# Three side steps per 18 gated products, a longer estimate for one load, and a weight set split in other places

## The chip, the core and the metric

The kernel runs on one core of one Trainium2 chip. The core has five engines that work side by side, each from its own queue, in order: TensorE (PE, matrix products; PEld is its weight load), VectorE (DVE), ScalarE (ACT), GpSimd (POOL) and SyncE (SP, which here issues transfers only). The metric is the device time of one execution in microseconds, the median of several runs; lower is better.

## The reference, cut

```python
# q, k, v: (4, 12, 448, 64)
scores = cap * np.tanh(q @ k.T / np.sqrt(64) / cap)
attn = np.exp(scores - scores.max(-1)); attn /= attn.sum(-1) + 1e-9
x = (attn @ v)                 # as (1792, 768)
x = ((x @ w1) * (x @ w2)) @ w3 @ w_out        # gated: w1, w2 768x1024, w3 1024x1024
h = x @ w_in                   # 768x1024
sm = softmax(h); solu = h * sm
ln = (solu - mean) / np.sqrt(var + 1e-6) * g_ln
out = ln @ w_out2              # 1024x768
```

All is float32. A product of two float32 numbers is made of three products of a high and a low half ("h", "l" in names): a cast makes the high half, a subtraction the low one. So every operand and weight tile has to be split before TensorE may use it.

## The kernel before

**Stages.** The attention runs over 24 pairs of heads (names sc, p, o, n). Beside it TensorE multiplies weights with weights: w3, w_out and w_in become one matrix, stored as w_dr (names f). Then come the gated products (names ab, wt, xs): for each of eight blocks f of the inner width, weights w_f come in three pieces (landing in ld, converted on VectorE by L328, L331, L334 into cv, cast by L340, the low half by L349), and tokens of four batches b are multiplied with them. The gated products begin beside the attention and go on after it. Six blocks of the gated products for the last two batches are made by a scheme of seven products for eight (L1332, names us, ys, vs; block n, product j; weights q). The last two stages use the same scheme for the folded matrix (L1432, weights ws, one tile for each of the seven sets; operands a) and for the output (weights wg).

**What sets the order.** In the attention a planner (class Order) writes the order of all engines: every step has an engine, a rank, a time on that engine and a time until its result is there, and is put in the queue when the planner's clock says so. Side work waits in two lists: `ahead` (weights) and `xq` (tokens). For the tokens, `plan_x` loads the row sums' inverses rb from DRAM by GpSimd (L830), VectorE scales by them (L843), the results are cast and split. The numbers behind `("pool", ...)` on the line that ends `plan_x` are the planner's time for the issue and until the load has landed, in ns.

After the attention the planner stops. The rest of the gated products runs in a plain loop: `fill(18 * 201)` gives TensorE 18 products, then `ahead.step(n)` takes n steps of the side list, `xq.step(1)` one of the tokens. This part alone is left to a scheduler, which orders what is recorded there by its own model. The blocks behind it are in a fixed order again: `plan(n, j, ...)` puts side work behind product j of block n. `finish` copies us to p1s, u2s, p7s on ScalarE (L1336) and adds on VectorE (L1339).

**Names of the change.** `EARLY` is the order (1, 2, 6, 7, 5) of the weight sets; `EARLY[1]` is set 2, tile ws2, loaded by `block_load` and split into high and low halves by `plan_block` (L340, L349) or by `high_w` and `low_w` (L1372, L1376). `high(r, m)` takes a buffer for operand m of row block r and makes the high half; for m of 3, 4 and 5 the buffers are three of one tag, dealt in the order in which they are asked for. They lie where tiles of the stage before lay, so the first use of each waits until its former tile is read.

Of the kernel before, what the change touches and what calls it, by code (L numbers as in the profile page):

```python
# [10 lines left out]
F32R = mybir.dt.float32r  # L11
# [7 lines left out]
P = 128  # L19
# [6 lines left out]
HALF = 512  # L26
# [17 lines left out]
EARLY, LATE = (1, 2, 6, 7, 5), (4, 3)  # L44
# [197 lines left out]
def attention_moe_solu(ctx: ExitStack, tc: tile.TileContext, q, k, v, cap, w12, w3t, wo, win, wout2, g_ln, out):  # L242
# [9 lines left out]
    pe, act, dve, pool, sync = nc.tensor, nc.scalar, nc.vector, nc.gpsimd, nc.sync  # L252
# [567 lines left out]
    def plan_x(b, parts=range(NPAIR // 2)):  # L820
        for part in parts:
            i = len(xq.items)
            pairs = slice(2 * part, 2 * part + 2)
            one, open_ = [], since(lambda b=b, part=part: free_x(b, part))

            def load(i=i, pairs=pairs):
                rb[i] = early.tile([P, 2, S], F32, tag="rb", name=f"rb{i}")
                for j in range(2):
                    row = r_dr[b].rearrange("(n j) s -> j n s", j=2)[j:j + 1, pairs]
                    pool.dma_start(out=rb[i][j * D:(j + 1) * D], in_=row.to_broadcast([D, 2, S]))  # L830

            def begin(part=part, one=one):

                for c in (2 * part, 2 * part + 1):
                    xs[b, c] = place_x(b, c)
                one.append(raw(xs[b, 2 * part + 1][:, 0, :1]))
                pool.memset(one[0], 1.0)

            def scale(i=i, part=part, one=one):
                two, *each = xr[b, part]  # L840
                by = rb.pop(i)
                for x, y in ([(two, by)] if two is not None else [(x, by[:, k]) for k, x in enumerate(each)]):
                    dve.scalar_tensor_tensor(x, x, one[0], y, ALU.mult, ALU.mult)  # L843

            def first(begin=begin, scale=scale):
                return [("pool", 0, 120, 300, begin), ("dve", 2, 1090, 1230, scale)]

            def rest(part=part):
                (_, *x), steps = xr.pop((b, part)), []
                if b == 3:  # L850
                    whole[part] = x
                for i in range(2):
                    to = xs[b, 2 * part + i]
                    steps.append(("any", 1, copying(S), None, lambda e, to=to, i=i: cast(to[:, 0], x[i], e)))
                for i in range(2):
                    to = xs[b, 2 * part + i]
                    steps.append(("dve", 2, 560, 680, lambda to=to, i=i: low(to[:, 0], to[:, 1], x[i])))
                slot = held_at.pop(("xr", b, part))
                return steps + [("none", 0, 0, 0, lambda: ring["xr"].give(slot, order.time))]

            def there(b=b, part=part, open_=open_):
                times = stored.get((b, part)), open_()
                return None if None in times else max(times)
            xq.add(("x", b, part), load, first, rest, None, there, ("pool", 1300, 5200))

# [45 lines left out]
    def block_load(m, part, dr, t_dr, dst):  # L913
        sync.dma_start(out=raw(dst[:, 1, rows(part), :]), in_=block_src(m, part, dr, t_dr))
# [5 lines left out]
    def second(m):  # L920
        if m not in ws:
            ws[m] = both_.tile([P, 2, NF // 2, HALF], F32R, tag="many", name=f"ws{m}")
        return ws[m]

    def plan_block(m, part):
        there = since(lambda: "ws" in place)
        ahead.add(("f", m, part), lambda: block_load(m, part, W4, tw_dr, second(m)), list,
                  lambda: [("none", 0, 0, 0, lambda: block_split(ws[m], part))], None, there)
# [79 lines left out]
    def plan_plain(key, do, test, load=lambda: None):  # L1008
        ahead.add(key, load, list, lambda: [("none", 0, 0, 0, do)], None, since(test))
# [64 lines left out]
    plan_tg(4, 5, 6, 7)  # L1074
    for c in range(NC // 2):
        plan_plain(("U", c), lambda c=c: one_four(c), lambda: (NF - 1, 1) in fin)
    for part in range(2):
        plan_block(EARLY[1], part)
    plan_plain("set1", lambda: None, lambda: (NF, PASSES[1][1]) in fin, lambda: load_set(1))

    def gated_tile(t):
# [221 lines left out]
    opened(right, "below", "right").tile([P, 16], F32, name="below")  # L1303
    place["set"], place["ts"] = opened(right, "set", "right"), opened(right, "ts", "right")
    while fill(18 * 201):
        ahead.step(2)
        xq.step(1)
    while xq.step(1):
        pass
# [7 lines left out]
    def plan(n, j, *entries):  # L1317
        for f, *args in entries:
            side.setdefault((n, j), []).append(lambda f=f, args=args: f(*args))
# [58 lines left out]
    for n in range(AGAIN):  # L1378
        follows = n + 1 < AGAIN
        if n:  # L1380
            plan(n, 0, (combine_low, n, 3))
        plan(n, 0, (low12, n, 6), (high12, n, 3))
        plan(n, 1, (low12, n, 7), (low12, n, 5), (low12, n, 3))
        if follows:
            plan(n, 2, (combine, n + 1, 7))
            plan(n, 3, (combine_low, n + 1, 7), (combine, n + 1, 5))
            plan(n, 4, (combine_low, n + 1, 5), (combine, n + 1, 6), (high12, n + 1, 7))
            plan(n, 5, (combine_low, n + 1, 6), (high12, n + 1, 5))
            plan(n, 6, (combine, n + 1, 3), (high12, n + 1, 6))
        if n + 2 < AGAIN:  # L1390
            for j, q in ((1, 0), (2, 1), (4, 2), (6, 3)):
                plan(n, j, (load_quarter, n + 2, q))
        plan(n, 6, (given, n, PASSES[1][0], "u2"))
    plan(LATER - 1, 0, (load_first,))
    plan(LATER, 0, (last_sets,), (load_ws, EARLY[2]), (load_ws, EARLY[3]))
    plan(LATER, 3, (first_operands,))
# [25 lines left out]
    side, both, taken = {}, {}, [2]  # L1422
# [119 lines left out]
    def source(r, m):  # L1542
        if m in (1, 6):
            return (x[r][0] if m == 1 else sums[r][2]).rearrange("p (a b) -> p a b", a=2)
        return {7: lambda: sums[0][3][:, HALF:], 5: lambda: sums[r][1], 4: lambda: quarter(r, 1, 1), 3: lambda: sums[r][4]}[m]()

    def high(r, m):
        if m in (1, 6, 7):
            t = op.tile([P, 2, 2, HALF], F32R, tag="two", bufs=3, name=f"a{r}_{m}")
            if m != 7:  # L1550
                a.setdefault(r, {}).update({m: t[:, 0], m + 1: t[:, 1]})
                both[r, m] = t[:, :, 0], t[:, :, 1]
            else:
                a[r][m] = t[:, 1]
                both[r, m] = t[:, 1, 0], t[:, 1, 1]
        else:
            a[r][m] = t = op.tile([P, 2, HALF], F32R, tag="one", bufs=3, name=f"a{r}_{m}")
            both[r, m] = t[:, 0], t[:, 1]
        act.copy(both[r, m][0], source(r, m))  # L1559

    def low(r, m):
# [51 lines left out]
        ws[EARLY[4]] = place["w567"].tile([P, 2, NF // 2, HALF], F32R, tag=f"w{EARLY[4]}", name=f"ws{EARLY[4]}")  # L1613

    plan(0, 0, (fifth,), (load_late, 5), (load_late, 4), (load_late, 3), (load, 1, 0), (load, 1, 1), (low_w, ws, 7, 0), (high_w, ws, 7, 1), (low_w, ws, 7, 1), (begun_sums,))
    plan(0, 1, (high, 0, 7), (low, 0, 7), (high, 0, 5), (low, 0, 5))
    plan(0, 3, (high_w, ws, 5, 0), (low_w, ws, 5, 0), (high_w, ws, 5, 1), (low_w, ws, 5, 1), (high, 0, 4), (high_w, ws, 4, 0), (sum4, 0))
    plan(0, 4, (low, 0, 4), (low_w, ws, 4, 0), (high_w, ws, 4, 1), (low_w, ws, 4, 1), (high, 0, 3), (high_w, ws, 3, 0))
    plan(0, 5, (low, 0, 3), (low_w, ws, 3, 0), (high_w, ws, 3, 1), (low_w, ws, 3, 1))
# [123 lines left out]
```

## Time and profile before

| | us |
|---|---|
| median of 3 runs (800.0 to 800.51) | 800.07 |
| the profiled execution, its own time | 805.94 |
| its span, first to last instruction | 804.2 |
| mean granted clock of TensorE, share of full speed | 0.985 |
| TensorE busy | 778.8 |
| VectorE busy | 617.6 |
| ScalarE busy | 440.8 |

The busy times come from one execution. TensorE's is close to the span, so a reader looks for the places where it stands still, and at the granted clock around them: after a pause TensorE may run at 1.2 instead of 2.4 GHz. Times in the rows below count from the span's start.

### The profile page before, as it was taken

Reading aid. Unit: us, or ns where it says so; the run is one execution under the profiler, and the core shown is the slowest. Engines: PE = TensorE matmul, PEld = TensorE weight load, DVE = VectorE, ACT = ScalarE, POOL = GpSimd, SP = SyncE. Lnnn points to the kernel's source line nnn. Section 1 sums busy time; section 2 is a strip of 40 time slices with the busy share of each in tenths; the row PEclk is TensorE's granted clock in tenths of the full one; section 3 lists DMA queues with packets and bytes.
Section 4 is the critical chain, followed back from the end, with each engine's and each line's share of the span. In section 5 each row is a group of like instructions: output and inputs, shape, how many; then the busy total and the mean of one; then the engine's idle time right before and its main releaser. Section 6 shows DMA issues by size and latency. Waiting matters only on the chain.

```text
span 804.2 us, 11305 instructions
## 1 busy us (share of the span) xinstructions
PE 778.8 (97%) x3956; PEld 617.6 (77%) x3956; DVE 617.6 (77%) x1134; ACT 440.8 (55%) x654; POOL 54.4 (7%) x106
## 2 busy tenths in 40 slices
PE   9999999999999998999986998999999999999998
PEld 6556666867766765777975997998688888899998
DVE  6995795799898668765776977787886668878973
ACT  6877766357487685672321312224576667755642
POOL 0110000001100111000100000000011111100000
PEclk9999999999999999999997998999999999999999
DMA  8776456677977765627968797463833335996532
GB/s 285 246 233 209 145 193 193 180 256 256 308 259 241 239 181 174 216 105 290 326 223 302 251 292 235 143 192 140 273 110 124 113 100 119 269 214 132 144 92 79
DMA packets 150936, 162.46 MB, mean 202 GB/s; under 512 B 66340, under 2 KB 122848, under 8 KB 149856
## 3 DMA queue, kind: packets, MB, share of 16 engines
q1 hardware_dynamic: 148144, 155.91, 61.2%
q0 software_dynamic: 2592, 5.73, 3.1%
q8 instruction: 31, 0.51, 0.3%
q14 instruction: 25, 0.20, 0.1%
q10 hardware_dynamic: 144, 0.10, 0.0%
HBM read 114.04 MB, written 47.53 MB: 201 GB/s over the span
## 4 chain that ended last, share of the span: by engine, by line
PE 74%; DMA 10%; DVE 8%; ACT 4%; issue 3%; SPq 0%; POOL 0%; DVEq 0%; ACTq 0%; POOLq 0%
PE u L1432 14%; PE ab L1120 8%; PE f L755 8%; PE o L523 7%; PE f L771 7%; PE v L1432 7%; PE sc L442 5%; PE us L1332 5%; PE y L1432 4%; DMA ld<-in_w 3%; PE vs L1332 2%; PE n L523 2%; PE sc L438 2%; DMA rb<-r_dr 2%; DMA tg_dr<-t 1%
## 5 line engine op out<-in xcount | busy, mean ns | idle before, releaser
L1120 PE MATMUL ab<-xs,wt 128*128 128x448 f32 x720 | 154.8, 374 | 10.1 <-ACT wt L340 9.8
L1120 PEld LDWEIGHTS ab<-xs,wt 128*128 128x128 f32 x720 | 138.7, 194 | 26.6 <-ACT wt L340 10.5
L455 ACT ACTIVATE sc<-sc,small 128x896 f32<-128x896 f32 (+1 forms) x96 | 82.8, 888 | 47.3 <-PE sc L442 40.6
L460 ACT ACTIVATE p<-sc,small 128x896 f32<-128x896 f32 (+1 forms) x96 | 84.3, 919 | 0.6
L1432 PE MATMUL u<-ws,a 128*128 128x512 f32 x336 | 80.8, 391 | 1.2 <-DVE ws L1376 0.9
L523 PE MATMUL o<-p,vd 128*64 128x448 f32 x384 | 77.5, 545 | 0.0
L1432 PEld LDWEIGHTS u<-ws,a 128*128 128x128 f32 x336 | 62.8, 188 | 15.6 <-DVE ws L1376 1.8
L755 PE MATMUL f<-w,w_o 128*128 128x512 f32 x288 | 70.6, 396 | 0.0
L771 PE MATMUL f<-w_i,w 128*128 128x512 f32 x288 | 68.6, 393 | 0.1
L755 PEld LDWEIGHTS f<-w,w_o 128*128 128x128 f32 x288 | 53.2, 188 | 16.3 <-issue 3.4
L771 PEld LDWEIGHTS f<-w_i,w 128*128 128x128 f32 x288 | 53.4, 188 | 15.0 <-issue 2.0
L1432 PE MATMUL u<-wg,a 128*128 128x384 f32 x336 | 62.1, 335 | 0.0
L1432 PEld LDWEIGHTS u<-wg,a 128*128 128x128 f32 x336 | 58.5, 188 | 0.4 <-DVE a L1563 0.2
L523 PEld LDWEIGHTS o<-p,vd 128*64 128x64 f32 x384 | 25.4, 136 | 41.2 <-issue 40.3
L334 DVE SCALAR_TENSOR_TENSOR cv<-ld,cv 128x512 uint32<-128x512 uint32 (+1 forms) x80 | 51.9, 659 | 0.6
L331 DVE SCALAR_TENSOR_TENSOR cv<-ld,cv 128x512 uint32<-128x512 uint32 (+1 forms) x80 | 51.8, 658 | 0.7
L1559 ACT CAST a<-s 128x512 fp32r<-128x512 f32 (+1 forms) x42 | 31.3, 754 | 33.6 <-DVE s L1581 18.1
L328 DVE TENSOR_SCALAR cv<-ld 128x512 uint32<-128x512 uint32 (+1 forms) x80 | 32.2, 406 | 14.1 <-DMA ld<-in_w 7.9
L1563 DVE TENSOR_TENSOR a<-s,a 128x512 fp32r<-128x512 f32 (+1 forms) x42 | 35.5, 851 | 9.5 <-ACT a L1559 9.4
L481 DVE TENSOR_TENSOR s<-p,p 128x896 f32<-128x896 f32 x18 | 19.6, 1089 | 29.2 <-ACT p L460 16.2
L1432 PE MATMUL v<-ws,a 128*128 128x512 f32 x168 | 40.7, 390 | 0.5 <-DVE ws L1376 0.5
L1432 PEld LDWEIGHTS v<-ws,a 128*128 128x128 f32 x168 | 31.5, 188 | 7.4 <-DVE ws L1376 0.9
(187 smaller groups left out, 1305.3 us busy)
## 6 DMA issues: line engine op xcount, KB each, us to landing
ld<-in_w SPq DMA_DIRECT2D x24, 512.0 KB, 4.5
w_dr<-wt SPq DMA_DIRECT2D x6, 1536.0 KB, 8.1
q<-w_dr SPq DMA_DIRECT2D x24, 384.0 KB, 3.8
ld<-in_w3t SPq DMA_DIRECT2D x16, 512.0 KB, 4.4
w_dr<-e SPq DMA_DIRECT2D x28, 256.0 KB, 3.8
ldx<-ab_dr SPq DMA_DIRECT2D x14, 512.0 KB, 4.1
c_dr<-h SPq DMA_DIRECT2D x14, 512.0 KB, 2.7
ldx<-c_dr SPq DMA_DIRECT2D x56, 128.0 KB, 3.2
```

The source lines that it names most:

```text
L331: dve.scalar_tensor_tensor(d[1], d[0][:, :, 1], 0xC0000000, d[1], ALU.bitwise_and, ALU.bitwise_or)
L334: dve.scalar_tensor_tensor(d[1], d[0][:, :, 0], 29, d[1], ALU.logical_shift_right, ALU.bitwise_or)
L442: pe.matmul(sc[:, j, :S], keys[rows], qq[rows, :], start=(m == 0), stop=(m == len(terms) - 1))
L455: act.activation(sc[:, :w, :S], sc[:, :w, :S], AF.Tanh, scale=qscale)
L460: act.activation(p, sc[:, :w, :S], AF.Exp, scale=capt)
L523: pe.matmul(dst[i * width:(i + 1) * width, :S], weights, moving, start=first, stop=stop)
L755: pe.matmul(banks_[c][0], lw[:, a], fw["3", h, g][:, e], start=begins, stop=(g == NF - 1 and m == 2))
L771: pe.matmul(begun_[m_][0], w34[m_][:, a, c, :], rw[:, e], start=(c == 0 and m == 0), stop=(c == NC - 1 and m == 2))
L1120: pe.matmul(pp[f, b, i][0][:, :S], w[:, u], xs[b, c][:, e], start=begins, stop=(c == NC - 1 and m == 2))
L1332: pe.matmul(pu[g], w[:, u, c * P:(c + 1) * P], moved(m, c)[:, e], start=(begins and c == 0 and i == 0), stop=(c == NC // 2 - 1 and i == 2) ...
L1432: pe.matmul(banks[g], a[r][m][:, p, k * P:(k + 1) * P], b[m][:, e, k, :], start=(first and k == 0 and i == 0), stop=(k == NF // 2 - 1 and ...
L1563: dve.tensor_tensor(lo, source(r, m), raw(hi), ALU.subtract)
```

## The change

Four edits:

- The planner's time until a load of rb has landed goes from 5200 to 9000 ns. Everything that it plans from the first of these loads on moves.
- The loop after the attention takes three steps of the side list for 18 products, not two.
- Set ws2 is loaded by one transfer instead of two, and no longer split where the list comes to it: its halves are cast behind product 3 of blocks n=1 and n=2, and the low halves follow behind product 4.
- The buffer of operand 4 of the first row block is taken before that of operand 5, by a new function `reserve`; the work itself stays where it was.

```diff
-            xq.add(("x", b, part), load, first, rest, None, there, ("pool", 1300, 5200))
+            xq.add(("x", b, part), load, first, rest, None, there, ("pool", 1300, 9000))
...
-    for part in range(2):
-        plan_block(EARLY[1], part)
+    plan_plain(("f", EARLY[1]), lambda: None, lambda: "ws" in place, lambda: block_load(EARLY[1], None, W4, tw_dr, second(EARLY[1])))
...
     while fill(18 * 201):
-        ahead.step(2)
+        ahead.step(3)
...
+    for part in range(2):
+        plan(1 + part, 3, (high_w, ws, EARLY[1], part))
+        plan(1 + part, 4, (low_w, ws, EARLY[1], part))
...
+    def reserve(r, m):
+        a[r][m] = op.tile([P, 2, HALF], F32R, tag="one", bufs=3, name=f"a{r}_{m}")
...
         else:
-            a[r][m] = t = op.tile([P, 2, HALF], F32R, tag="one", bufs=3, name=f"a{r}_{m}")
-            both[r, m] = t[:, 0], t[:, 1]
+            if m not in a[r]:
+                reserve(r, m)
+            both[r, m] = a[r][m][:, 0], a[r][m][:, 1]
...
-    plan(0, 1, (high, 0, 7), (low, 0, 7), (high, 0, 5), (low, 0, 5))
+    plan(0, 1, (reserve, 0, 4), (high, 0, 7), (low, 0, 7), (high, 0, 5), (low, 0, 5))
```

VectorE in the attention, before, where the inverse of the row sums of pairs 16 and 17 (inv17) is made; the load rb8 that follows on GpSimd reads what comes of it, and L843 with rb7 is the scaling before:

```order
L603 TENSOR_SCALAR inv17_2907<-inv17_2907,small_70 112x16
L843 SCALAR_TENSOR_TENSOR many_81<-many_81,xs2_3_2982,rb7_2921 128x448
L843 SCALAR_TENSOR_TENSOR xr2_1_2521<-xr2_1_2521,xs2_3_2982,rb7_2921 128x448
L608 RECIPROCAL inv17_2907<-inv17_2907 112x16
L349 TENSOR_TENSOR ql20_2999<-qd20_2931,qh20_2998 128x448
```

After, from the scaling with rb6 on; the one with rb7 comes 15 rows behind the reciprocal:

```order
L843 SCALAR_TENSOR_TENSOR many_81<-many_81,xs2_1_2993,rb6_2901 128x896
L603 TENSOR_SCALAR inv17_2930<-inv17_2930,small_70 112x16
L349 TENSOR_TENSOR ql20_2976<-qd20_2916,qh20_2975 128x448
L1138 TENSOR_TENSOR abs_0_1_3017<-ab1_0_1_2964,a_0_1_2983 128x448
L608 RECIPROCAL inv17_2930<-inv17_2930 112x16
```

The reciprocal L608 has moved from behind the scaling with rb7 to well before it.

VectorE in the gated products after the attention, before, from the first to the third piece of w6 (landed in ld73, ld74, ld75; the tile is wt6):

```order
L328 TENSOR_SCALAR cv73_3885<-ld73_3815 128x512
L331 SCALAR_TENSOR_TENSOR cv73_3885<-ld73_3815,cv73_3885 128x512
L334 SCALAR_TENSOR_TENSOR cv73_3885<-ld73_3815,cv73_3885 128x512
L328 TENSOR_SCALAR cv74_3893<-ld74_3842 128x512
L331 SCALAR_TENSOR_TENSOR cv74_3893<-ld74_3842,cv74_3893 128x512
L349 TENSOR_TENSOR wt6_3884<-cv73_3885,wt6_3884 128x512
L334 SCALAR_TENSOR_TENSOR cv74_3893<-ld74_3842,cv74_3893 128x512
L328 TENSOR_SCALAR cv75_3922<-ld75_3852 128x512
L349 TENSOR_TENSOR wt6_3884<-cv74_3893,wt6_3884 128x512
L331 SCALAR_TENSOR_TENSOR cv75_3922<-ld75_3852,cv75_3922 128x512
L1139 TENSOR_TENSOR abs_5_1_4031<-ab1_5_1_3992,a_5_1_3990 128x448
L334 SCALAR_TENSOR_TENSOR cv75_3922<-ld75_3852,cv75_3922 128x512
```

After, the same number of rows from the same place (many and xs3 are tokens of the last batch; abs is a finished product):

```order
L328 TENSOR_SCALAR cv73_3889<-ld73_3788 128x512
L331 SCALAR_TENSOR_TENSOR cv73_3889<-ld73_3788,cv73_3889 128x512
L334 SCALAR_TENSOR_TENSOR cv73_3889<-ld73_3788,cv73_3889 128x512
L843 SCALAR_TENSOR_TENSOR many_81<-many_81,xs3_5_3795,rb11_3742 128x896
L349 TENSOR_TENSOR wt6_3888<-cv73_3889,wt6_3888 128x512
L1018 TENSOR_TENSOR many_81<-many_81 128x448 x2
L349 TENSOR_TENSOR xs3_4_3794<-many_81,xs3_4_3794 128x448
L349 TENSOR_TENSOR xs3_5_3795<-many_81,xs3_5_3795 128x448
L1138 TENSOR_TENSOR abs_5_1_4039<-ab1_5_1_4020,a_5_1_4018 128x448
L328 TENSOR_SCALAR cv74_3897<-ld74_3821 128x512
L331 SCALAR_TENSOR_TENSOR cv74_3897<-ld74_3821,cv74_3897 128x512
L328 TENSOR_SCALAR cv75_3905<-ld75_3831 128x512
```

The scaling with rb11 and five instructions behind it now stand between the first and the second piece.

ScalarE at the first block of seven products, before (n=0: p1s0, u2s0, p7s0):

```order
L1336 COPY p1s0_4649<-us0_4637 128x448
L340 CAST ws2_4486<-ws2_4486 128x1024
L1336 COPY u2s0_4680<-us0_4637 128x448
L340 CAST ws2_4486<-ws2_4486 128x1024
L1336 COPY p7s0_4697<-vs0_4682 128x448
L983 CAST q0_1_4535<-s7_1_4675 128x384
```

After, up to the next block's p7s1:

```order
L1335 COPY p1s0_4644<-us0_4632 128x448
L1335 COPY u2s0_4675<-us0_4632 128x448
L1335 COPY p7s0_4692<-vs0_4677 128x448
L983 CAST q0_1_4538<-s7_1_4670 128x384
L983 CAST q1_1_4629<-s5_1_4688 128x384
L983 CAST q1_1_4629<-s63_1_4704 128x384 x2
L1335 COPY p1s1_4750<-us1_4737 128x448
L1335 COPY u2s1_4781<-us1_4737 128x448
L1371 CAST ws2_4447<-ws2_4447 128x1024
L1335 COPY p7s1_4799<-vs1_4783 128x448
```

The two casts of ws2 have left the first block; one stands between u2s and p7s of the second, the other likewise in the third.

## Rows read from the trace of the kernel before

**Rows 1.** The page: busy time, share of the span, instructions of each engine.

```profile
PE 778.8 (97%) x3956; PEld 617.6 (77%) x3956; DVE 617.6 (77%) x1134; ACT 440.8 (55%) x654; POOL 54.4 (7%) x106
```

**Rows 2.** Waits of TensorE, whole span: engine, line, awaited, us, times, longest.

```profile
PE ab L1120 <- ACT wt L340: 9.8, 2, 7.2
PE us L1332 <- ACT u2s L1336: 3.9, 1, 3.9
PE sc L438 <- ACT p L460: 3.0, 2, 2.3
...
PE u L1432 <- DVE ws L1376: 0.9, 2, 0.5
```

**Rows 3.** Stretches of 20 us: length, busy (instructions) per engine, PEclk, DMA share, GB/s.

```profile
300.00:320.00 20.00, 17.73 (x96) 11.17 (x93) 17.64 (x31) 12.06 (x18) 2.53 (x5) 0.93 0.60 184
...
400.00:420.00 20.00, 17.14 (x77) 15.22 (x76) 16.23 (x30) 6.12 (x11) 0.00 (x0) 0.91 0.66 230
420.00:440.00 20.00, 12.76 (x52) 11.40 (x51) 12.77 (x27) 2.28 (x4) 0.00 (x0) 0.74 0.88 304
...
480.00:500.00 20.00, 16.09 (x66) 14.43 (x66) 15.42 (x32) 5.35 (x10) 0.00 (x0) 0.83 0.79 254
```

**Rows 4.** TensorE in time: start, length, line, count, idle before and releaser.

```profile
316.61 0.47 PE L438 MATMUL sc<-ql,kh 128*128 128x448 f32 x1 [2.27 <-ACT p L460]
...
431.59 45.99 PE L1120 MATMUL ab<-xs,wt 128*128 128x448 f32 x216 [7.25 <-ACT wt L340]
...
481.02 1.96 PE L1332 MATMUL us<-t,q 128*128 128x448 f32 x9
482.82 1.97 PE L1332 MATMUL vs<-t,q 128*128 128x448 f32 x9
488.70 3.73 PE L1332 MATMUL us<-t,q 128*128 128x448 f32 x9 [3.91 <-ACT u2s L1336]
492.23 3.18 PE L1332 MATMUL vs<-t,q 128*128 128x448 f32 x9
```

**Rows 5.** GpSimd, VectorE, ScalarE around one load of rb; then all of rb.

```profile
304.18 1.20 POOL L830 DMA_DIRECT2D rb<-r_dr  x2 [3.66 <-DMA r_dr<-inv]
...
311.64 1.15 DVE L843 SCALAR_TENSOR_TENSOR many<-many,xs,rb 128x896 f32<-128x896 f32 x1 [2.15 <-DMA rb<-r_dr]
...
312.82 0.56 ACT L340 CAST xs<-many 128x448 fp32r<-128x448 f32 x1 [4.39 <-DVE many L843]
...
  DMA rb<-r_dr: 8.4, 4
DMA to landing us min/median/max: 3.7/5.5/9.3
```

**Rows 6.** SyncE and VectorE in time, at the loads of w6 and w7.

```profile
389.69 0.35 SPq L318 DMA_DIRECT2D ld<-in_w  x1
...
404.90 0.43 DVE L328 TENSOR_SCALAR cv<-ld 128x512 uint32<-128x512 uint32 x1 [2.82 <-DMA ld<-in_w]
...
422.87 0.37 SPq L318 DMA_DIRECT2D ld<-in_w  x1
```

**Rows 7.** ScalarE, then VectorE in time, first blocks after the gated products.

```profile
487.17 1.04 ACT L340 CAST ws<-ws 128x1024 fp32r<-128x1024 f32 x1 [7.16 <-DMA ws<-w_dr]
...
484.69 0.62 DVE L1339 TENSOR_TENSOR p1s<-ys,p1s 128x448 f32<-128x448 f32 x1
...
488.25 1.22 DVE L349 TENSOR_TENSOR ws<-ws 128x1024 fp32r<-128x1024 f32 x1 [0.21 <-ACT ws L340]
...
490.99 0.55 DVE L975 TENSOR_TENSOR s<-s,q 128x384 f32<-128x384 f32 x1
...
506.30 0.62 DVE L1339 TENSOR_TENSOR p7s<-us,p7s 128x448 f32<-128x448 f32 x1 [1.11 <-PE us L1332]
```

**Rows 8.** ScalarE, then VectorE in time, first block of the last stage.

```profile
569.29 0.62 ACT L1559 CAST a<-s 128x512 fp32r<-128x512 f32 x1 [3.05 <-PE u L1432]
...
571.37 2.36 DVE L1376 TENSOR_TENSOR ws<-ws 128x1024 fp32r<-128x1024 f32 x2
```

## The prediction, made blind

> **What bounds the kernel now.** I read the page first. TensorE is busy for 778.8 us of a span of 804.2 [rows 1], so 25.4 us are left in which it does nothing, and the changed program has the same TensorE instructions, piece for piece (3642 matmul rows before and after). Nothing that this change does can shorten TensorE's work; it can only take away idle time, and the half clock that follows idle time. So the second view is what TensorE waited for, over the whole span. The reader is to see in [rows 2] that four places make up most of what has a name: 9.8 us in two waits for a cast of gated weights, one of 7.2 and so one of 2.6; 3.9 us once for the copy of u2s; 3.0 us in two waits of the scores for an exponential, the longer 2.3; and 0.9 us in two waits for the low half of a weight set in the first block of the last stage.
>
> The third view is the granted clock in stretches of 20 us [rows 3]. It is full elsewhere; it is 0.93, 0.91, 0.74 and 0.83 in the stretches that hold these waits. TensorE ran at 1.2 instead of 2.4 GHz for a while after each of the long ones. A wait therefore costs more than its idle time. After the wait of 2.27 us [rows 4] the stretch shows 0.93, which is 7% of 20 us, 1.4 us lost. After the wait for u2s, nine matmuls took 3.73 and the next nine 3.18 us, against 1.97 for nine before it [rows 4]: 1.76 and 1.21, together 3.0 us lost.
>
> **The change part by part, first the longer estimate.** The plan that lays out the attention stretch believed that the row sums rb land 5.2 us after their issue; now it believes 9.0. Shown: the issues took 3.7 to 9.3 us to land, 5.5 in the middle, and VectorE stood waiting for them four times, 8.4 us in all [rows 5]. One of these made the larger score wait. GpSimd issued rb at 304.18; VectorE, idle for 2.15, could scale with it at 311.64, 7.5 us later; ScalarE's cast of the result, at 312.82, had waited 4.39; behind that cast in ScalarE's queue stood the tanh and exponential that TensorE wanted, and it got them at 316.61 [rows 4, 5]. The order shows why the load was late: the reciprocal of the row sums stood behind the scaling with the load before it, and now stands 15 rows ahead of it. With 9.0 us allowed, VectorE has other work in front of the scaling. I take both score waits as gone, 3.0 us [rows 2], and the 1.4 us of half clock [rows 3]: 4.4. From about 170 us on the whole stretch is planned anew, though, and I leave 0.4 us for small new waits. Term: 4.0. Bounds: 4.4, and below nothing, since a new plan can hold a new wait of the same kind (the slower rival).
>
> The Trainium skill speaks against this term: "DMA: Bandwidth & Descriptors", section "Anatomy of one DMA — SWDGE (gpsimd) path", fits a transfer issued by GpSimd as 2.0 us and its bytes at 436 GB/s. An estimate from it for the 224 KB of an rb half is 2.5 us, under the old 5.2; by that the term would be 0. The measured 5.5 and 9.3 above decide; the case has a chance below.
>
> **Three side steps for two.** This acts after the attention, in the gated products, where a scheduler still orders what is recorded. So the step count itself shows little: SyncE's queue holds the same loads of the weights w6 and w7 with the same stores ahead of them, but for three places. The loads of the first set of w_f (ws1) now stand ahead of the sums' loads; the stores of the sums stand ahead of the second piece of w6 instead of behind it; and VectorE scales the last tokens (L843) and does five instructions more between the first and the second piece of w6. The waits there are set by a chain of transfers: the first piece of w6 was issued at 389.69 and VectorE had it at 404.90, 15.2 us later; the first of w7 was issued at 422.87, and TensorE went on with it at 431.59, 8.7 us later [rows 4, 6]. The bytes ahead of w6 in SyncE's queue are the same, so I expect it at the same time. In the better case it lands up to 3 us sooner, since fewer stores run beside it. In the worse, the second piece's conversion stands behind one L843 of 1.15 us [rows 5] and five instructions of some 0.62 [rows 7], 4.2 us. TensorE takes 24 matmuls from the first piece before it wants the second, 4.8 us at 1.80 us for nine (482.82 less 481.02 [rows 4]), which covers that; but the load of w7 comes behind that conversion, and I bound what it loses by the same 4.2 us. Term: 0, from a gain of 3 to a loss of 4.
>
> **The second weight set split within the blocks.** Shown: ScalarE waited 7.16 us for the load of ws2 to land, cast half of it from 487.17 [rows 7], and only then copied u2s, for which TensorE waited 3.91 us until 488.70 [rows 4]. In the new order both casts are gone from there and stand in the blocks of n=1 and n=2. That gives back 3.9 and the 3.0 of half clock, 6.9. What is late next is VectorE. It added p1s at 484.69, and at 490.99 began the last step (0.55) before it could add p7s [rows 7]. 6.3 and 0.55 us, less the two ws2 instructions of 1.22 each and a wait of 0.21 for them [rows 7] that leave this place, make 4.2, so p7s is added from 488.9 to 489.5, 0.62 later; TensorE wants it after three groups of nine from 482.82, at 488.2. It will wait some 1.3 us. The trace has half clock after 2.27 us; whether 1.3 brings it too I cannot read from these rows, and it would cost up to the same 1.4; I take nothing, and keep the other end for the range. Term: 6.9 less 1.3, 5.6, from 4.2 to 6.9. In n=1 and n=2 the moved VectorE instruction (1.22) falls where VectorE waited 1.11 us for TensorE [rows 7], and ScalarE's cast falls between two copies for which it waits for TensorE: nothing, as long as that cover holds; without it up to 1.2 us each.
>
> **First buffers dealt anew.** In the first block of the last stage the cast of the fifth operand waited 3.05 us for TensorE at 569.29 [rows 8], since its buffer lay on an operand that was still being read. Now the fourth operand, due later, takes that buffer, and the wait for TensorE is gone from the cast in the order with its waits. The low halves of the sets follow on VectorE, without a pause from 571.37 [rows 8]; each ends half a microsecond too late for TensorE. What moves up is that row: its cast stands on ScalarE behind a copy that waits for the same product of TensorE, and that copy no longer has the late cast's own 0.62 us in front of it [rows 8]. Term: 0.6; bounds 0 and the 0.9 us of the two waits [rows 2].
>
> **Sum.** 4.0, 0, 5.6 and 0.6 are 10.2 us of the profiled execution. Its own time is 805.94, of which 804.2 is the span; the median of the runs is 800.07, 5.87 less. If these 5.87 us are all in waits, a wait is 23% shorter in the runs timed, and 7.9 us come off; if they lie elsewhere, 10.2. I take the middle, 9.1: 791.0 us, 787.5 to 793.5 with both ends.
>
> **The rivals.** *w6 and w7 come later*: the loss of 4 above, 795. For it: two more queued things in front of each. Against: w7's chain has slack wherever SyncE, not VectorE, was last. *They come sooner*, by 3 and less half clock after it: 787 or below. *The estimate buys nothing*, rb landing within 5.2 us in the runs timed, which have no profiler beside them: 9.1 less 4.0, 795.0. It is what the Trainium skill's "DMA: Bandwidth & Descriptors", named above, would give. *No change that can be measured* (0.2%, 1.6 us; about what a measurement of this kernel can tell): that, and one new wait in the attention stretch of the size seen, 2.3 with 1.4 of half clock: 798.7. *Slower*: one mechanism, the plan made anew. If casts for the gated products stand in ScalarE's queue ahead of an exponential and what they want is late, TensorE waits as at 316.61, 3.7 us with its half clock. With the term of 4.0 lost it decides from the second such wait on: 795.0 and 7.4 are 802.4, and three are 806. For it: two of the scores waited so before [rows 2]. Against: a longer estimate puts more work, not less, in front of each scaling, and two are all that the attention showed.
>
> **How the numbers follow.** Forecast 0.55; w6 and w7 later 0.17; sooner 0.09; the estimate buys nothing 0.07; no change 0.05; slower 0.07. Time 791.0. The range 786.0 to 797.5 takes in the forecast, both cases at 795 and half of the sooner one, some 0.83. Faster by over 0.2%: 0.88; within: 0.05; slower: 0.07.
>
> **What would show it.** Right, if TensorE's waits no longer hold u2s and the exponentials, a wait of about a microsecond for p7s stands instead, the clock is full from 300 to 340 us and 0.9 or more in the first blocks after the gated products, and the two waits for wt are still some 10 us. Wrong, if VectorE still waits for rb by several microseconds, if the waits for wt grow or vanish, or if scores wait for ScalarE elsewhere in the attention.

## The result, and the profile after

The changed kernel takes 794.47 us (median of 4 runs, 793.56 to 796.17), the kernel before 800.29 in the same comparison: 0.9915 times as long, 95% interval 0.9886 to 0.9943. It is faster, by under 1%: 5.8 us between the medians, 6.8 us (4.6 to 9.1) by the ratio; 791.0 was predicted, with a range of 786.0 to 797.5. The ratios and intervals here are estimates on record over all the runs, not quotients of two medians (which would be 0.9927 here), and gains in us read in the two ways differ by up to 1.5. The profiled execution shows more, a span of 792.3 us where that of before was 804.2. Both numbers have to be explained.

TensorE's row of the page of the changed kernel, to be read against [rows 1]:

```profile
PE 772.7 (98%) x3956; PEld 613.7 (77%) x3956; DVE 617.1 (78%) x1132; ACT 442.3 (56%) x656; POOL 55.0 (7%) x106
```

A span of 792.3 less 772.7 busy leaves 19.6 us in which TensorE does nothing, against 25.4 before. That is 5.8 of the 11.9 us. The other 6.1 is busy time, 778.8 less 772.7, with as many matmuls (x3956 in both): the price of the half clock, and the mean granted clock has gone from 0.985 to 0.993.

What TensorE waited for in the changed kernel, as [rows 2] (engine, line, awaited, us in all, times, longest):

```profile
PE ab L1119 <- ACT wt L340: 8.3, 2, 6.3
PE vs L1331 <- ACT p7s L1335: 2.8, 1, 2.8
...
PE sc L438 <- ACT p L460: 0.5, 1, 0.5
```

u2s (3.9 us) has gone from the list and the exponential is down from 3.0 to 0.5 (at another place, 263.18, where ScalarE had waited 5.00 us for a store of other weights and not for an rb). The wait for wt stands at 8.3, and a new one stands behind it: 2.8 us for p7s, awaited from ScalarE.

The stretches of 20 us, as [rows 3] (length, busy per engine, granted clock, DMA share, GB/s):

```profile
300.00:320.00 20.00, 20.00 (x115) 12.97 (x112) 19.08 (x33) 14.61 (x21) 2.58 (x5) 1.00 0.60 198
...
400.00:420.00 20.00, 16.25 (x72) 14.67 (x72) 16.47 (x33) 5.20 (x9) 0.00 (x0) 0.91 0.74 252
420.00:440.00 20.00, 15.68 (x67) 14.48 (x68) 16.07 (x34) 5.49 (x10) 0.00 (x0) 0.83 0.87 306
...
480.00:500.00 20.00, 18.11 (x91) 16.98 (x91) 16.20 (x31) 6.75 (x13) 0.00 (x0) 1.00 0.65 214
```

The clock is full in the first and the last of them, where it was 0.93 and 0.83. It is still down after the two waits for wt, 0.91 and 0.83.

The places of [rows 4] again, TensorE in time (start, length, line, count, idle before and releaser):

```profile
313.82 0.47 PE L438 MATMUL sc<-ql,kh 128*128 128x448 f32 x1
...
317.04 0.47 PE L442 MATMUL sc<-ql,kh 64*128 64x448 f32 x2
...
401.80 16.25 PE L1119 MATMUL ab<-xs,wt 128*128 128x448 f32 x72 [2.01 <-ACT wt L340]
...
424.32 45.76 PE L1119 MATMUL ab<-xs,wt 128*128 128x448 f32 x216 [6.28 <-ACT wt L340]
...
469.93 1.96 PE L1331 MATMUL us<-xs,q 128*128 128x448 f32 x9
...
477.13 1.97 PE L1331 MATMUL us<-t,q 128*128 128x448 f32 x9
481.89 2.07 PE L1331 MATMUL vs<-t,q 128*128 128x448 f32 x9 [2.79 <-ACT p7s L1335]
...
487.40 1.96 PE L1331 MATMUL ys<-xs,q 128*128 128x448 f32 x9
```

The scores of 316.61 begin at 313.82 and wait for nothing. The two waits for wt are 2.01 and 6.28 us. In the first block, nine matmuls into us follow each other, then 2.79 us go by until the copy of p7s is made. Three of these rows stand for places that are measured from below; before, they were:

```profile
321.19 0.47 PE L442 MATMUL sc<-ql,kh 64*128 64x448 f32 x2
...
477.42 1.96 PE L1332 MATMUL us<-xs,q 128*128 128x448 f32 x9
...
498.84 1.96 PE L1332 MATMUL ys<-xs,q 128*128 128x448 f32 x9
```

The first is the score group behind the wait of 316.61, the second the first product of the first block, the third the second product of the next block.

The load of rb in that part of the attention, GpSimd's issue, VectorE's scaling with it, and then what the rb loads were waited for and how long they took, as [rows 5]:

```profile
309.01 1.67 POOL L830 DMA_DIRECT2D rb<-r_dr  x2 [8.92 <-DVE xr L843]
...
318.65 1.15 DVE L843 SCALAR_TENSOR_TENSOR many<-many,xs,rb 128x896 f32<-128x896 f32 x1
...
  DMA r_dr<-inv: 2.6, 1
DMA to landing us min/median/max: 3.4/6.0/8.2
```

The loads land no sooner than before, 6.0 us in the middle against 5.5. But VectorE comes for this one 9.6 us after its issue, without a pause, and no instruction waits for the landing of an rb any more (the one wait for a transfer that is left in this view is for the store ahead of it).

### The profile page after: what moved, and what is told of

The parts are those of the page before. It is cut to its first block, busy times and chain, and to the rows that moved or that the text cites. A ratio compares the mean times of both kernels' runs of the same rounds, so it can differ in the third digit from the quotient of the medians.

```text
span 792.3 us, 11304 instructions
## 1 busy us (share of the span) xinstructions
PE 772.7 (98%) x3956; PEld 613.7 (77%) x3956; DVE 617.1 (78%) x1132; ACT 442.3 (56%) x656; POOL 55.0 (7%) x106
## 4 chain that ended last, share of the span: by engine, by line
PE 76%; DMA 9%; DVE 8%; ACT 4%; issue 2%; SPq 0%; DVEq 0%; ACTq 0%
PE u L1434 14%; PE o L523 9%; PE f L771 8%; PE f L755 8%; PE ab L1119 7%; PE v L1434 7%; PE sc L442 6%; PE us L1331 5%; PE y L1434 4%; PE n L523 2%; PE sc L438 2%; PE vs L1331 2%; DMA ld<-in_w 2%; DMA tg_dr<-t 2%; DMA ws<-w_dr 1%
## 5 line engine op out<-in xcount | busy, mean ns | idle before, releaser
L1119 PE MATMUL ab<-xs,wt 128*128 128x448 f32 x720 | 152.7, 370 | 8.3 <-ACT wt L340 8.3
L523 PEld LDWEIGHTS o<-p,vd 128*64 128x64 f32 x384 | 25.4, 136 | 41.2 <-issue 40.3
L481 DVE TENSOR_TENSOR s<-p,p 128x896 f32<-128x896 f32 x18 | 19.6, 1091 | 32.8 <-ACT p L460 18.1
```

The costliest lines, as they stand in the source:

```text
L523: pe.matmul(dst[i * width:(i + 1) * width, :S], weights, moving, start=first, stop=stop)
L1119: pe.matmul(pp[f, b, i][0][:, :S], w[:, u], xs[b, c][:, e], start=begins, stop=(c == NC - 1 and m == 2))
```

## Where the new wait comes from

SyncE's queue, then ScalarE, at the start of the first block:

```profile
472.83 0.58 SPq L914 DMA_DIRECT2D ws<-w_dr  x1
473.50 0.64 SPq L1147 DMA_DIRECT2D ab_dr<-abs  x1
...
475.53 0.54 ACT L1335 COPY u2s<-us 128x448 f32<-128x448 f32 x1 [3.01 <-PE us L1331]
481.30 0.53 ACT L1335 COPY p7s<-vs 128x448 f32<-128x448 f32 x1 [5.24 <-DMA ab_dr<-abs]
```

ScalarE copied u2s as soon as its product was there, which is what the change was to allow. It would then copy p7s out of vs, but stood 5.24 us until a *store* had landed: ab_dr<-abs. L1334 and the order of the buffers tell why. p7s of the first block takes its buffer from the ring of two that the last products of the gated stage (abs) use; u2s takes the other. The store of the last abs was issued at 473.50, right behind the 1 MB load of ws2, and landed just before 481.30, 7.8 us later.

In the kernel before the same copy used the same buffer, and did not wait (SyncE, then ScalarE):

```profile
483.15 0.53 SPq L1148 DMA_DIRECT2D ab_dr<-abs  x1
...
489.66 0.53 ACT L1336 COPY p7s<-vs 128x448 f32<-128x448 f32 x1
```

There the store of the last abs, issued at 483.15 behind the two half loads of ws2 (481.23), had 6.5 us before ScalarE came, since the split of ws2 and u2s kept it until 489.66. Up to that much the store cost nothing. The change took this cover away with the wait for u2s.

## Experiments: the four edits alone

Each of these is the kernel before with one of the four edits of the change and nothing else. The lines that decide, of the first, second, third and fourth:

```diff
+            xq.add(("x", b, part), load, first, rest, None, there, ("pool", 1300, 9000))
...
+        ahead.step(3)
...
+    plan_plain(("f", EARLY[1]), lambda: None, lambda: "ws" in place, lambda: block_load(EARLY[1], None, W4, tw_dr, second(EARLY[1])))
...
+        plan(1 + part, 3, (high_w, ws, EARLY[1], part))
+        plan(1 + part, 4, (low_w, ws, EARLY[1], part))
...
+    plan(0, 1, (reserve, 0, 4), (high, 0, 7), (low, 0, 7), (high, 0, 5), (low, 0, 5))
```

| kernel | median us | before, same chip | ratio | 95% interval |
|---|---|---|---|---|
| estimate alone | 797.77 | 802.97 | 0.9939 | 0.9917 to 0.9961 |
| three steps alone | 802.55 | 802.97 | 0.9995 | 0.9981 to 1.0009 |
| ws2 alone | 800.58 | 802.97 | 0.9968 | 0.9949 to 0.9987 |
| buffers alone | 802.28 | 802.97 | 0.9994 | 0.9976 to 1.0011 |

> The kernel before with one edit, the estimate for rb at 9000 in place of 5200. Whole sum to be shared out: the median fell by 5.8 us (800.3 to 794.5), the profiled span by 11.9, of which the two traces lay 4.2 at this edit's place (scores up to 321 us). Theory A, each place's share of the span holds in the runs timed at half its size: 2.0 us off the median, 798.3, and in this profile no wait of TensorE for an exponential above 1 us. Theory B, the profiled execution of the kernel before was 5.9 us above its median because rb and w6/w7 happened to land late in it: this edit gives 0 to 0.5, 799.8 to 800.3, and the four waits of VectorE for rb are short in both.

Measured, the estimate alone takes off 0.6%, 4.9 us (3.1 to 6.7). That is above what either theory allowed. Its waits of TensorE, then the landing of rb:

```profile
PE ab L1120 <- ACT wt L340: 10.4, 3, 6.7
...
PE sc L438 <- ACT p L460: 0.7, 1, 0.7
...
DMA to landing us min/median/max: 3.5/6.2/8.5
```

One wait of 0.7 for an exponential is left, and VectorE waits for no rb, though the landings are as long as before. So the gain isn't an accident of the execution profiled; the three other kernels of this table, which keep the old number, still show 2.8 to 3.7 us of score waits and 7.8 to 8.5 us of VectorE waiting for rb. Theory B falls. So does the halving in theory A, for this edit. The 4.9 us lie in two places, and only one of them is that of the scores. In the profiles of the four kernels with 5200 the score group behind the wait begins at 318.5 to 321.8 us, in seven executions with 9000 at 316.1 to 317.5. From there to the first block it takes 153.9 to 156.2 us with 5200 and 151.7 to 153.2 with 9000, whether the loop takes two steps or three; this one, with two, takes 153.2.

> The kernel before with one edit, three side steps in place of two. The traces showed 3.3 us less lost at the two waits for wt (10.1 to 8.3 us of idle, the rest half clock). Theory A: half of it, 1.6 us off the median, 798.7. Theory B: 0 to 0.5, so 799.8 to 800.3. My prediction had 0 here, from a gain of 3 to a loss of 4. In the trace: the two waits for wt at 8.3 us if the step count is their cause, 10 if it was the other edits that moved them.

TensorE's waits for wt and for an exponential in it:

```profile
PE ab L1120 <- ACT wt L340: 9.5, 2, 8.8
...
PE sc L438 <- ACT p L460: 2.8, 2, 1.8
```

Ratio 0.9995: nothing, or at most 1.5 us by the interval. The waits for wt are 9.5 us in all, within their scatter (below). Theory A's share for this place, 1.6 us, falls, by little.

> The kernel before with one edit, the second weight set loaded in one piece and split within the blocks. The traces showed 4.0 us gained between the first product of the first block and the second block: the wait for u2s (3.9) and its half clock (3.0) gone, a wait of 2.8 for the copy of p7s new, which ended with the landing of a store of abs. Theory A, at half size: 2.0 off the median, 798.3. Theory B: this place is the one that counts, 4 to 5 off, 795.3 to 796.3. In the trace of either: no wait for u2s, and one of 2 to 3 us for p7s, if one load of 1 MB right ahead of the store of abs is what holds it back.

Its waits of TensorE:

```profile
PE ab L1119 <- ACT wt L340: 9.6, 2, 7.4
PE sc L438 <- ACT p L460: 3.0, 2, 2.3
PE vs L1331 <- ACT p7s L1335: 2.8, 1, 2.8
```

The wait for u2s is gone and the 2.8 us for p7s are there, in the kernel with this edit alone. It gains 2.6 us (1.0 to 4.1); theory A's 2.0 lies well within that, theory B's 4 to 5 at its end or beyond.

> The kernel before with one edit, the reserved buffer in the first block of the last stage. The two traces showed four waits of TensorE of 0.3 to 0.5 us there before and three after, 0.5 us less. Theory A and B alike: 0.2 to 0.6 off the median, 799.7 to 800.1, which is within what a measurement can tell from none; its trace shows one wait for ws fewer and no wait of 3 us of ScalarE for TensorE at the cast of the fifth operand.

Of its waits of TensorE, the one for ws on u:

```profile
PE u L1432 <- DVE ws L1376: 0.5, 1, 0.5
```

It is one fewer than before [rows 2], as expected; ScalarE no longer waits 3 us there for its cast. The ratio, 0.9994, can't be told from no change.

The product of the four ratios is 0.9896. To see whether they add up, the changed kernel was run once more, and beside it two ways to take the new wait away.

> The changed kernel as it is, for the other three to be held against. The four edits alone gave ratios of 0.9939, 0.9995, 0.9968 and 0.9994, whose product is 0.9896. If they add up, the ratio here is 0.988 to 0.992. If the estimate and the weight set gain the same thing (each hides what the other leaves), it is nearer 0.994.

794.9 us against 803.35, ratio 0.9910 (0.9880 to 0.9941). The four edits add up as far as this can tell. The changed kernel's median is within 0.4 us of the first comparison; it is the kernel before that moved, with medians of 800.29, 802.97, 803.35 and 802.11 in four comparisons. So the medians give 5.8 us in the first comparison and 8.5 in this one; by the ratios the two agree, 6.8 and 7.2 us.

## Experiments: the wait for p7s

The copy in another ring:

```diff
-        keeps[name] = place["ab"].tile([P, S], F32, tag="a" if name == "p1" else "ab", bufs=2, name=f"{name}s{n}")
+        keeps[name] = place["ab"].tile([P, S], F32, tag="ab" if name == "u2" else "a", bufs=2, name=f"{name}s{n}")
```

> The changed kernel with the copy p7s in the ring of buffers that p1s uses, not in the one of u2s and abs; the order of instructions on every engine is the same. Theory: the new wait of 2.8 us is p7s's buffer, still being stored as abs. Then that wait goes, the copy follows its product within a microsecond, and what is left is VectorE's add for p7s, 1 us or less; the median falls by 1.5 to 2.8 us against the changed kernel, ratio to the kernel before lower by 0.002 to 0.0035. Rival: ScalarE's own queue or VectorE is late there anyway, the wait for p7s turns into one for the add or for u2s of over 2 us, and the ratio stays within 0.001.

791.92 us, ratio 0.9877 (0.9844 to 0.9909), 3.0 us below the changed kernel on the same chip. TensorE, VectorE and ScalarE in time:

```profile
480.55 3.88 PE L1331 MATMUL us<-xs,q 128*128 128x448 f32 x18 [1.17 <-DVE p7s L1338]
...
479.40 0.56 DVE L975 TENSOR_TENSOR s<-s,q 128x384 f32<-128x384 f32 x1
479.88 0.61 DVE L1338 TENSOR_TENSOR p7s<-us,p7s 128x448 f32<-128x448 f32 x1
...
475.86 0.54 ACT L1335 COPY p7s<-vs 128x448 f32<-128x448 f32 x1 [1.31 <-PE vs L1331]
```

ScalarE copies p7s after 1.31 us of idle time, and it is TensorE's product that ends it. What TensorE now waits for is VectorE's add, 1.17 us: at 479.40 VectorE is still at the last step in front of it. This is the wait that the prediction had here, and nearly its size (1.3).

The load behind the store:

```diff
-    plan_plain(("f", EARLY[1]), lambda: None, lambda: "ws" in place, lambda: block_load(EARLY[1], None, W4, tw_dr, second(EARLY[1])))
...
+    plan(0, 0, (lambda m: block_load(m, None, W4, tw_dr, second(m)), EARLY[1]))
```

> The changed kernel with the 1 MB load of ws2 issued in the first block, behind the last store of abs, not right ahead of it. Theory of the queue: the store took 7.7 us because 1 MB stands ahead of it; now it lands in 3 to 5 us, the wait for p7s falls from 2.8 to under 1 us, the ratio falls by 0.002 to 0.003. Rival: the store is slow because 16 engines are full of other loads (share of DMA 1.01 from 460 to 480 us); it still takes 6 us or more, the wait stays over 1.5 us, and the ratio moves by under 0.0015.

791.87 us, ratio 0.9869 (0.9843 to 0.9896), 3.0 us below the changed kernel on the same chip; the ratio is 0.004 lower, where 0.002 to 0.003 was expected. SyncE, ScalarE, TensorE:

```profile
473.01 0.56 SPq L1146 DMA_DIRECT2D ab_dr<-abs  x1
473.66 0.61 SPq L914 DMA_DIRECT2D ws<-w_dr  x1
...
477.92 0.54 ACT L1334 COPY p7s<-vs 128x448 f32<-128x448 f32 x1 [1.27 <-PE vs L1330]
...
481.32 3.76 PE L1330 MATMUL us<-xs,q 128*128 128x448 f32 x18
```

The store now stands at 473.01 ahead of the load, and ScalarE's copy at 477.92 waits for TensorE, not for it: it had landed within 4.9 us, against 7.8 behind the load (6.2 to 7.8 in the six executions in which it stood behind the load and ScalarE waited for it). The megabyte right ahead of the store was what held it back. The stretch from 460 to 480 us, with the load ahead (the changed kernel) and with the load behind:

```profile
460.00:480.00 20.00, 19.09 (x96) 17.51 (x94) 15.06 (x39) 3.73 (x7) 0.00 (x0) 1.00 1.01 321
...
460.00:480.00 20.00, 20.00 (x102) 18.72 (x101) 16.39 (x42) 5.52 (x11) 0.00 (x0) 1.00 1.04 328
```

The DMA share was 1.01, and it is 1.04 with the load behind; the rival, that full engines alone make the store slow, is refuted.

Both edits together:

> The changed kernel with both edits that took the wait for p7s away: its copy in the other ring, and the load of ws2 behind the last store of abs. Each alone left 0 or 1.2 us of waits there (ratios 0.9869 and 0.9877). Theory: both cure one cause, so nothing adds up, ratio 0.985 to 0.988, within 0.0015 of the load alone. Rival: the moved load had a gain of its own besides (ws2 out of the way of the operands' loads), and the two together reach 0.984 or less.

TensorE in time, where the wait for p7s was:

```profile
481.35 3.88 PE L1330 MATMUL us<-xs,q 128*128 128x448 f32 x18 [1.34 <-DVE p7s L1337]
```

791.68 us, ratio 0.9863 (0.9832 to 0.9895). Nothing adds up, as expected of two cures for one cause. What is left is VectorE's add again, 1.34 us; with the load alone it was hidden, since the block began later there (470.52 against 469.04 and 468.41) and VectorE's add hardly did (480.19 against 479.88 in the other ring). The medians of all three are some 3 us under the changed kernel's, for this one that of the changed kernel with two steps (794.92, below), since it ran on another chip; which is the fastest of them can't be told.

One length sums up the place: from the first product of the first block (us) to the second of the next (ys), eight groups of nine matmuls. Without a wait it is 14.40 us, the load moved later. The kernel before took 21.42, the changed kernel 17.47 and 16.54 in its two profiles, the other ring 15.85, both edits 16.03. The prediction's term of 5.6 would have made it 15.82.

## Experiments: the estimate and the steps in the changed kernel

The estimate at 13000, and at 7000 below:

```diff
-            xq.add(("x", b, part), load, first, rest, None, there, ("pool", 1300, 9000))
+            xq.add(("x", b, part), load, first, rest, None, there, ("pool", 1300, 13000))
```

> The changed kernel with the estimate for rb at 13000 in place of 9000. Theory: 9.0 us already covers the landings (3.4 to 8.2 us in the changed kernel, no wait of VectorE for rb left), so more gives nothing: VectorE waits for rb 0 us, the ratio within 0.002 of the changed kernel's, or higher by up to 0.004 where casts come too late for the gated products. Rival: the gain comes from having the attention stretch planned anew, whatever the number; then this plan is another one and may come out 3 us to either side while VectorE's waits for rb are 0 in both.

796.01 us, ratio 0.9921 (0.9892 to 0.9950): no more than with 9000. The wait of VectorE for rb, then waits of TensorE:

```profile
  DMA rb<-r_dr: 2.4, 1
...
PE ab L1119 <- ACT wt L340: 10.6, 3, 9.9
...
PE sc L438 <- ACT p L460: 1.3, 1, 1.3
```

The theory isn't quite borne out. VectorE waits for an rb once again, 2.4 us, and a score waits 1.3, behind a cast of queries (qh) whose load came 3.84 us late: a still larger number is another plan, and the plan has its own small accidents.

> The changed kernel with the estimate for rb at 7000, between 5200 and 9000. Theory, the number has to cover the landing (median 6, longest 8 to 9.5 us, the same before and after): loads of more than 7 us still make VectorE wait, one or two waits and 1 to 4 us in all (8 in four or five waits at 5200, none at 9000), and the ratio is 0.991 to 0.995. Rival, any new plan of the stretch gains: no relation to the number, VectorE's waits for rb either none or as long as at 5200.

798.33 us, ratio 0.9943 (0.9918 to 0.9967). The changed kernel had 0.9910, and with two steps it has 794.92 us and 0.9898 on the chip of this run (below). The intervals overlap a little; by the medians 3.4 us are lost. ScalarE and TensorE in time, then VectorE's wait for rb:

```profile
233.40 0.57 ACT L340 CAST qh<-qd 128x448 fp32r<-128x448 f32 x1 [4.38 <-DMA qd<-in_q]
...
236.72 0.74 PE L438 MATMUL sc<-ql,kh 128*128 128x448 f32 x1 [3.29 <-ACT p L460]
...
  DMA rb<-r_dr: 5.5, 3
```

VectorE waits 5.5 us in three waits, between the 8.4 in four at 5200 and the none at 9000, in the order that the theory has, though more than the one or two waits and the 4 us that were expected. But the score's wait of 3.29 us in this kernel is of another kind. ScalarE had a cast of the next queries (qh) in its queue ahead of the exponential, and the load of those queries (qd) came 4.38 us late. It is of the kind that the prediction gave as the slower rival, an early cast that waits for its data in front of an exponential, though there it was a cast for the gated products. It is real; it was only not in the plan that 9000 makes. And it is TensorE's only wait for an exponential from 100 to 380 us in this profile: none of the three waits for rb held up TensorE. So this run doesn't show that the rest of the waits for rb cost those 3.4 us, nor does it refute the rival, that any new plan of the stretch moves the time by what it happens to bring. That late rb loads hold up TensorE is shown at 5200, where both score waits of the kernel before stand behind such a cast (the wait of 0.71 us at 286.94 behind one that had waited 3.68).

Two steps in the changed kernel:

```diff
-        ahead.step(3)
+        ahead.step(2)
```

> The changed kernel with two side steps again, the other three edits kept. My prediction gave the step count 0, from a gain of 3 to a loss of 4, and alone it moved nothing (ratio 0.9995). Theory: it moves nothing here either, ratio within 0.002 of the changed kernel's 0.991, the waits for wt at 8 to 10 us. Rival: only with the shorter attention stretch does the third step pay, and without it the waits for wt are over 11 us and the ratio 0.994 or more.

Its waits for wt:

```profile
PE ab L1119 <- ACT wt L340: 8.2, 3, 5.9
```

794.92 us, ratio 0.9898 (0.9865 to 0.9932). The third step does nothing in either surrounding. The waits for wt are 8.2 us here, with two steps, and they were 8.3 and 9.4 in the two profiles of the changed kernel and 8.1 with the other ring, all with three steps: this place scatters by a microsecond from one execution to the next.

## Why the prediction was right, step by step

**What bounds the kernel.** That only idle time and the half clock behind it could go was right, and they went in about equal parts (5.8 and 6.1 us of the profiled execution).

**The estimate, 4.0.** Right in the mechanism at the scores, and about right in size there: 4.15 us between the two profiles, 3.4 in the mean between the kernels with 5200 and with 9000. Alone it gives 4.9 us (3.1 to 6.7), and that this is so near to 4.0 is partly luck, since about 2.5 us of the gain in the profiles come behind the scores, where the term had nothing. The half clock of the first wait was read a little small: the stretch from 320 to 340 us isn't full, as the prediction says, but 0.98, another 0.4 us. The loads weren't faster, VectorE had other work in front of them. The rival that it buys nothing is refuted by the estimate's run alone. The rule of the Trainium skill, page "DMA: Bandwidth & Descriptors", section "Anatomy of one DMA — SWDGE (gpsimd) path", gave an estimate of 2.5 us for this load; the changed kernel's loads took 3.4 to 8.2, so here it doesn't hold. The DMA engines were 60% busy in the stretch of the load at 309.01; whether that is the reason, no run shows.

**Three steps, 0.** Right: 0.9995 alone, and nothing with two steps in the changed kernel. The two profiles do differ by 3.3 us at this place (the first block begins at 469.93, not 477.42, so 7.49 us earlier, and 4.15 of that is there at the scores that begin at 321.19 before and at 317.04 after). Since two steps in the changed kernel show the same waits for wt, the step count isn't what made them shorter. The profiles point to the other plan of the attention: this stretch is shorter in all seven executions with 9000 than in any of the four with 5200, by 2.5 us in the mean (152.6 against 155.1), and 0.8 of the 3.3 us is then scatter. The prediction put nothing here for the estimate; how the plan does it, no run shows.

**The second weight set, 5.6.** This is the term that was mis-sized. In the profile, 21.42 less 17.47 is 3.95; alone, 2.6 us are measured (1.0 to 4.1). The 6.9 that were to be given back (the wait for u2s and its half clock) were given back. The step that failed is "what is late next is VectorE": VectorE was, by the 1.17 us that the other ring shows against 1.3 predicted, but a store was later still. The prediction followed the engines and not the buffers. It looked at the buffer of the fifth operand in the last stage, but didn't ask whose buffer p7s takes, nor when the store from it lands. Both could be seen beforehand: the line that makes p7s names the ring of abs, and the store stands in SyncE's queue right behind the load of ws2. The 2.8 us of wait brought no half clock; the prediction had taken none for its 1.3.

**First buffers, 0.6.** Alone the ratio is 0.9994 (0.9976 to 1.0011). The trace bears out the mechanism (one wait fewer, no late cast); the size is below what can be measured.

**The sum.** 10.2 was predicted for the profiled executions, 11.9 came: 4.15, 3.3, 3.95 and 0.5 by place, where 4.0, 0, 5.6 and 0.6 stood. Two errors, one each way, cancel in part: the stretch behind the scores gave 3.3 where nothing stood, the weight set 1.65 less. That the sum is so near is luck. The kernel before was also profiled in an execution 5.9 us above its median, so its side of these places may be on the high side. For the median, 9.1 was predicted, and 6.8 and 7.2 were found by the ratios of two comparisons (5.8 and 8.5 by the medians). As a ratio, 0.9887 was predicted, 0.9915 and 0.9910 were measured, and with the store's wait removed 0.9877 and 0.9869. The far end of the sum, 787.5, isn't quite what its bounds give: 4.4, 0, 6.9 and 0.9 are 12.2, and 800.07 less 12.2 is 787.9.

**The slower rival** didn't occur in this plan; at 7000 one wait of its kind did, 3.3 us, behind a cast of queries, and it didn't make the kernel slower than before.

## What to carry to other kernels

When an edit removes a wait, ask for the next operation on that engine not only which engine feeds it but whose buffer it writes into, and when the last transfer out of that buffer lands; a store that was harmless under the old wait is the new one. A large load is best issued behind a small store that somebody needs soon, not ahead of it: here that order alone was worth 0.4%. A planner's estimate for a transfer is better near the longest landing that the trace shows than near the middle, as long as there is other work to put in front: here 9.0 beat 5.2, with landings of up to 9.3 us. Beyond that, another number is only another plan (13.0 gained no more), and a plan made anew moves waits in places that the number has nothing to do with; look for them over the whole stretch that it orders.

## What was unexpected of the hardware

The half clock does not follow from the length of the idle time. Both of these stretches hold waits about as long as some that brought it elsewhere. The first is the estimate alone, with waits of 2.62 and 1.04 us for wt in the stretch, the second the three steps alone, with 1.77 us for an exponential (the wait, then its stretch):

```profile
402.48 5.29 PE L1120 MATMUL ab<-xs,wt 128*128 128x448 f32 x24 [2.62 <-ACT wt L340]
...
400.00:420.00 20.00, 15.18 (x72) 13.27 (x72) 17.22 (x34) 5.19 (x9) 0.00 (x0) 1.00 0.71 236
```

```profile
315.52 0.47 PE L438 MATMUL sc<-ql,kh 128*128 128x448 f32 x1 [1.77 <-ACT p L460]
...
300.00:320.00 20.00, 18.23 (x106) 11.20 (x102) 17.88 (x31) 12.24 (x18) 2.02 (x4) 1.00 0.61 176
```

Both show 1.00, where the kernel before shows 0.91 after a wait of 2.54 us for wt (at 407.48) and 0.93 after 2.27 [rows 3, 4], and the changed kernel shows 0.91 after 2.01 and 1.00 after the 2.79 of p7s. A term for half clock behind a wait of two to three microseconds is therefore an either-or, and belongs in the range rather than in the sum.

One kernel was far steadier than the rest. On one chip, the kernel before ran from 798.2 to 805.3 us in twelve runs, the changed kernel from 793.4 to 798.0 in six, and the one with the load moved later from 791.6 to 792.4 in six. With the other ring besides, on another chip, six runs took 790.8 to 794.3. With the other ring alone, on the first chip, they took 791.0 to 795.2, though the store's wait was gone there too; so that wait alone doesn't explain the spread, and what does wasn't found.
